# A fused attention, mixture-of-experts and bilinear kernel: heads grouped as 4 g + j, fewer small vector operations, and the attention's stores moved from SyncE's queue to ScalarE's

## The chip, the cores and the metric

The kernel runs on one core of one Trainium2 chip. The metric is the device time of one execution in microseconds (us). All tensors stay in the chip's memory; there is one launch. The core has five engines that run their own instruction streams in order: PE (TensorE), DVE (VectorE), ACT (ScalarE), POOL (GpSimd) and SP (SyncE, which issues DMAs and computes nothing). ACT and POOL can issue DMAs too; an issue stands in the stream of the engine that makes it.

## The reference, cut to what matters

Three stages follow one another; the diff touches the first.

```python
# 1. attention between x (8 batches, 8 heads, 512 rows, 64) and state (8, 8, 32, 64), both ways
scores = x @ state.T / 8;      xread = softmax(scores) @ state      # softmax over the 32 state rows
scores2 = state @ x.T / 8;     sread = softmax(scores2) @ x         # softmax over the 512 x rows
rows = concat([xread, sread], axis=2).transpose(0, 2, 1, 3).reshape(8 * 544, 512)   # heads side by side
# 2. mixture of experts: 8 experts, top 1, d_model 512, d_ff 1024
logits = rows @ w_gate;  e = argmax(logits);  p = softmax(logits)[e];  g = sigmoid(rows @ w_output_gate)[e]
y = p * g * (relu(rows @ w1[e]) @ w2[e])
# 3. bilinear layer
out = ((y @ wa) * (y @ wb)) @ w3 @ w_out
```

A softmax divides by its sum plus 1e-9.

## The kernel before

**Layout.** The 8 heads are split as h = 2 j + g, with g in 0..1 and j in 0..3: 4 heads of one g stand on the 128 partitions as 4 groups of 32 state rows. `st_n` holds the state so, `stT` its transposes, and `st_d` a block-diagonal form of it with 2 x 8 gate columns at its end, so that one product gives a row's attention result and its gate logits at once.

**One batch** is made of two functions. `softmaxes(b)` transposes x (PSUM tiles `pxT`, copied to `xT`), makes both score matrices (`psT`, taken over to `sT` with a running maximum `m2e`), transposes the scores (`pS`), subtracts the maximum of each 32 (`m1`, giving `a`), takes the exponentials (`a` and `a2`, both on ACT), sums them (`s1`, `s2`) and inverts the sums (`s1`, `r2`); POOL multiplies `a` by `s1` into `an`. `read(b)` transposes `a2` and `an` (`pa2T`, `paT`, copied to `a2T`, `aT`), makes the state's read (`psr`, scaled by `r2` into `sr`, stored to `x_rows`) and, for 4 chunks of 128 rows and 2 values of g, one product `pxr` of 272 columns: 256 are the attention result, copied to `xr` and stored, and 16 are logits, copied (g = 0) or added (g = 1) into `L` by DVE.

**What else runs beside it.** The weights `w3` and `w_out` arrive as 64-bit floats and are turned into 32-bit words by `convert`: ACT (L225, L239), DVE (L228, L230, L233) and POOL (L240); the raw words have a ring of 3 buffers (`RAW = 3`). Then `fuse` multiplies w3 by w_out, a block of 128 rows at a time: transposes `pw3`, split into a high and a low part (`w3T0`, `w3T1`), 24 products `pwo`. Blocks 0 to 2 are fused inside the attention, 3 to 7 beside the routing, where POOL makes the low parts.

**After the attention**, `route` (DVE, some 100 small operations) turns the logits `L` into expert slots and places; its first product is `pc`. POOL then gathers rows of `x_rows` (`xg`, L997), which are transposed (`pxg`) and go into the first expert unit (`ph4`, tiles 20 to 23).

**What sets the order.** A scheduler that is part of the language orders each engine's instructions from its own forecast of times, and picks the engine of an operation that is marked `any`: the copies `xr` (all of them), `xT` (three of four), and `aT`, `a2T` (one piece of the four) are so marked; the others are fixed. So an edit moves copies between ACT and DVE without the diff saying so. `bank` gives PSUM tiles from three tags, A (4), B (2) and C (2).

Lines of the profile before: L140 is `cp` (all copies), L548 `psT`, L556 the take-over of `sT`, L600, L606, L607 the small steps around `r2`, L632 `psr`, L654 `pxr`, L660 and L662 the logits, L643 and L663 the two stores, L328 the load of x, L208 the load of raw weights, L183 the products of `fuse` and of all later stages.

Of the kernel before, what the change touches and what calls it, by code (L numbers as in the profile page):

```python
# [52 lines left out]
def tile_attention_moe_bilinear(  # L53
# [256 lines left out]
    with ExitStack() as c1:  # L310
# [12 lines left out]
        def load_x(b):  # L323

            t = xin.tile([P, H, NC_, D], F32, tag="x", name=f"x{b}")
            for j in range(NJ):
                h = slice(2 * j, 2 * j + 2)
                eng("q_x", j, "sync").dma_start(  # L328
                    out=t[:, h].rearrange("p h c d -> p h (c d)"),
                    in_=x[b, h].rearrange("h (p c) d -> p h (c d)", c=NC_),  # L330
                )
            x_t[b] = t
# [4 lines left out]
        def load_state(b, n, qs):  # L337
            for h in range(H):
                j, g = divmod(h, 2)
# [29 lines left out]
        nc.scalar.dma_start(out=wg[:, :, 0:E], in_=w_gate.rearrange("(k p) e -> p k e", p=P))  # L369
        nc.scalar.dma_start(out=wg[:, :, E:], in_=w_ogate.rearrange("(k p) e -> p k e", p=P))  # L370
# [10 lines left out]
        def spread_state(b, n):  # L381
            for h in range(H):
                j, g = divmod(h, 2)
# [140 lines left out]
        def softmaxes(b):  # L524
# [3 lines left out]
            for j in range(NJ):  # L528
# [12 lines left out]
            s2 = two.tile([P, 2], F32, tag="s2", name=f"s2{b}")  # L541
            r2 = two.tile([P, 2], F32, tag="r2", name=f"r2{b}")

            t = [bank((kn("t_psT", "B")*4)[e], f"psT{b}_{e}") for e in range(2)]
            for j in range(NJ):
                for g in range(2):
                    for e in range(2):
                        nc.tensor.matmul(  # L548
                            t[e][at(j), g * S // 2 : (g + 1) * S // 2], stT[e ^ g][of(e), b, at(j)],
                            xT[of(e), 2 * j + g, :], start=True, stop=True,  # L550
                        )
            if kn("m2", 1):
                m2e = two.tile([P, 2, 2], F32, tag="m2e", name=f"m2e{b}")
                for g in range(2):
                    for e in range(2):
                        nc.vector.tensor_scalar(  # L556
                            sT[:, g].rearrange("p (c e n) -> p c e n", e=2, n=P)[:, :, e, :],
                            t[e][:, g * S // 2 : (g + 1) * S // 2].rearrange("p (c n) -> p c n", n=P),
                            1.0, None, op0=ALU.mult, op1=ALU.max, accum_out=m2e[:, e, g : g + 1],
                        )  # L560
                nc.vector.tensor_tensor(m2, m2e[:, 0], m2e[:, 1], op=ALU.max)
            else:
                for e in range(2):
                    cp(
                        "e_sT", e, sT.rearrange("p g (c e n) -> p g c e n", e=2, n=P)[:, :, :, e, :],
                        t[e].rearrange("p (g c n) -> p g c n", g=2, n=P),
                    )
                for g in range(2):
                    nc.vector.tensor_reduce(m2[:, g : g + 1], sT[:, g, :], axis=AX.X, op=ALU.max)
# [3 lines left out]
            for g in range(2):  # L573
                t = bank((kn("t_pS", "B")*4)[g], f"pS{b}_{g}")
                for c in range(NC_):
# [4 lines left out]
                nc.vector.tensor_reduce(m1[:, g], tv, axis=AX.X, op=ALU.max)  # L580
                nc.vector.tensor_tensor(
                    a[:, g], tv, m1[:, g].unsqueeze(2).to_broadcast([P, NC_ * NJ, NS]),
                    op=ALU.subtract,
                )
            av = a.rearrange("p g h n -> p (g h) n")
            nc.scalar.activation(av, av, AF.Exp, scale=SCALE)
            s1 = two.tile([P, 2 * NC_ * NJ], F32, tag="s1", name=f"s1{b}")
            nc.vector.tensor_reduce(s1, av, axis=AX.X, op=ALU.add)
# [3 lines left out]
            for g in range(2):  # L592
                eng("e_an", g, "gpsimd").tensor_tensor(
                    an[:, g].rearrange("p c (j n) -> p (c j) n", n=NS), a[:, g],
                    s1[:, g * NC_ * NJ : (g + 1) * NC_ * NJ]
# [3 lines left out]
            nm2 = two.tile([P, 2], F32, tag="nm2", name=f"nm2{b}")  # L599
            nc.vector.tensor_scalar_mul(nm2, m2, -SCALE)  # L600
            for g in range(2):
                nc.scalar.activation(
                    a2[:, g, :], sT[:, g, :], AF.Exp, bias=nm2[:, g : g + 1], scale=SCALE,
                    accum_out=s2[:, g : g + 1],
                )
            nc.vector.tensor_scalar_add(r2, s2, 1e-9)  # L606
            nc.vector.reciprocal(r2, r2)  # L607
# [15 lines left out]
        def read(b):  # L623
# [4 lines left out]
            for g in range(2):  # L628
                a2T = transposed(f"a2T{b}_{g}", [a2[:, g, c * P : (c + 1) * P] for c in range(NC_)], g)
                for c in range(NC_):  # L630
                    for j in range(NJ):
                        nc.tensor.matmul(  # L632
                            t[at(j), of(g)], a2T[:, c, at(j)], xt[:, 2 * j + g, c, :],
                            start=(c == 0), stop=(c == NC_ - 1),
                        )
            if b % 4 == 0:
# [6 lines left out]
            eng("q_sr", 0, "sync").dma_start(  # L643
                out=x_rows[b * R + S : (b + 1) * R, :].rearrange("n (j f) -> j n f", j=NJ), in_=sr
            )

            aT = [transposed(f"aT{b}_{g}", [an[:, g, c, :] for c in range(NC_)], 2 + g) for g in range(2)]
            xo = x_rows[b * R : b * R + S, :].rearrange("(p c) f -> c p f", c=NC_)
            for c in range(NC_):
                xr = xin.tile([P, DM], F32, tag="xr", name=f"xr{b}_{c}", bufs=kn("b_xr", 3))  # L650
                logits = L[:, b * NC_ + c]
                for g in range(2):
                    t = bank((kn("t_pxr", "CB")*8)[2 * c + g], f"pxr{b}_{c}_{g}")[:, 0 : NJ * D + 2 * E]
                    nc.tensor.matmul(t, aT[g][:, c, :], st_d[:, b % (B // 2), g], start=True, stop=True)  # L654
# [919 lines left out]
```

## Time and profile before

| | |
|---|---|
| median of 3 runs | 1168.14 us (1165.36 to 1170.16) |
| the profiled execution | 1171.04 us, its span 1169.1 us |
| PE busy | 1118.7 us (96%) |
| DVE, ACT, POOL busy | 664.0, 450.7, 398.2 us |
| granted TensorE clock, mean | 0.99 |

The span runs from the first to the last instruction of one execution. An engine is busy while it runs an instruction; the time in which an instruction waits inside itself counts as busy too. In a group of instructions the second last figure is the busy time and the mean of one in ns, the last the idle time just before them and what ended most of it.

### The profile page before, as it was taken

The numbers are of one execution on the slowest core, as the hardware profiler recorded it, in microseconds if no ns is written. First come the engines' busy times: TensorE is split into PE (matmuls) and PEld (weight loads), VectorE is DVE, ScalarE is ACT, GpSimd is POOL, SyncE is SP. The second block draws the span as 40 slices with busy tenths as digits, with TensorE's granted clock in tenths as the row PEclk, the third lists the DMA queues.
The fourth block names the chain that finished last, engine by engine and source line by source line (L and its number), as shares of the span: only waits on it lengthen the run. The fifth ranks groups of instructions, "written<-read, shape, count | busy, mean of one in ns | idle before, by whom it ended". The sixth has DMA issues, their size and how long they took to land. (4 is left out here: it accounts for less than half of the span.)

```text
span 1169.1 us, 18224 instructions
## 1 busy us (share of the span) xinstructions
PE 1118.7 (96%) x6880; PEld 982.7 (84%) x6880; DVE 664.0 (57%) x1206; ACT 450.7 (39%) x807; POOL 398.2 (34%) x383
## 2 busy tenths in 40 slices
PE   6888998999999999999999999999999999999995
PEld 4666777999999999987888888898888889889994
DVE  4999787636464546464855547343644545463341
ACT  3778644435454545454413223121412322131121
POOL 2555326114140322132001434623543453344222
PEclk9899999999999999999999999999999999999998
DMA  7786425546566666677414645443544445343431
GB/s 227 223 254 200 160 96 209 201 153 228 187 228 211 215 216 201 233 221 242 158 35 176 248 152 199 171 174 141 205 174 160 156 180 189 135 181 132 184 127 57
DMA packets 85008, 211.55 MB, mean 181 GB/s; under 512 B 12976, under 2 KB 42672, under 8 KB 79920
## 3 DMA queue, kind: packets, MB, share of 16 engines
q1 hardware_dynamic: 62256, 167.53, 42.2%
q10 hardware_dynamic: 17024, 24.42, 5.7%
q0 software_dynamic: 5632, 18.35, 4.5%
q8 instruction: 56, 0.92, 0.3%
q14 instruction: 40, 0.33, 0.1%
HBM read 166.23 MB, written 44.04 MB: 180 GB/s over the span
## 5 line engine op out<-in xcount | busy, mean ns | idle before, releaser
L183 PE MATMUL p<-w_x,w 128*128 128x448 f32 (+1 forms) x1638 | 338.6, 360 | 0.0
L183 PEld LDWEIGHTS p<-w_x,w 128*128 128x128 f32 x1638 | 303.7, 188 | 25.4
L183 PE MATMUL py<-h,w 128*128 128x288 f32 (+1 forms) x1152 | 197.9, 329 | 3.0 <-ACT y L1087 3.0
L183 PE MATMUL ph<-x,w 128*128 128x288 f32 (+2 forms) x1248 | 196.5, 316 | 2.9 <-DVE h L1025 2.7
L183 PEld LDWEIGHTS ph<-x,w 128*128 128x128 f32 x1248 | 179.4, 188 | 15.6 <-DVE h L1025 4.4
L183 PEld LDWEIGHTS py<-h,w 128*128 128x128 f32 x1152 | 173.8, 188 | 19.2 <-ACT y L1087 4.6
L178 DVE TENSOR_TENSOR w<-raw,w 128x1024 fp32r<-128x1024 f32 x80 | 96.9, 1237 | 74.6 <-ACT w L177 72.5
L1434 POOL TENSOR_TENSOR ab<-u,s 128x448 f32<-128x448 f32 (+1 forms) x40 | 47.6, 1189 | 259.3 <-DVE u L1432 170.4
L183 PE MATMUL po<-w_wo,aa 128*128 128x512 f32 x480 | 125.3, 393 | 1.9 <-ACT aa L177 1.0
L183 PEld LDWEIGHTS po<-w_wo,aa 128*128 128x128 f32 x480 | 89.7, 188 | 18.8 <-DVE aa L178 1.7
L177 ACT CAST w<-raw 128x1024 fp32r<-128x1024 f32 x80 | 81.6, 1050 | 51.6 <-DMA raw<-in_moe_w 46.8
L177 ACT CAST ab<-ab 128x384 fp32r<-128x384 f32 (+1 forms) x40 | 19.7, 493 | 184.4 <-POOL ab L1440 174.0
L240 POOL TENSOR_TENSOR wab<-wab,wab_top 128x512 int32<-128x512 int32 x16 | 20.7, 1292 | 179.5 <-DVE wab_top L233 151.5
L183 PE MATMUL po<-w_wo,ab 128*128 128x512 f32 x336 | 79.6, 391 | 0.4 <-DVE o L1466 0.4
L183 PEld LDWEIGHTS po<-w_wo,ab 128*128 128x128 f32 x336 | 62.9, 188 | 13.9 <-DVE o L1466 0.8
L997 POOL DMA_INDIRECT xg<-x_rows,gidx x38 | 45.7, 1202 | 83.3 <-PE pxg L1003 66.7
L1437 DVE TENSOR_TENSOR u<-u,p 128x448 f32<-128x448 f32 (+1 forms) x40 | 24.3, 606 | 84.4 <-PE p L183 84.3
L1438 POOL TENSOR_TENSOR ab<-u,s 128x448 f32<-128x448 f32 (+1 forms) x40 | 48.3, 1208 | 49.2 <-DVE u L1437 49.2
L1025 DVE SCALAR_TENSOR_TENSOR h<-ph,h 128x288 fp32r<-128x288 f32 (+2 forms) x104 | 51.2, 502 | 20.8 <-ACT h L1024 20.3
L1024 ACT ACTIVATE h<-ph 128x288 fp32r<-128x288 f32 (+2 forms) x104 | 44.5, 447 | 42.6 <-PE ph L183 30.8
L183 PE MATMUL pwo<-wu,w3T 128*128 128x512 f32 x192 | 50.2, 411 | 3.4 <-POOL w3T L178 2.9
L1440 POOL TENSOR_TENSOR ab<-ab 128x448 f32<-128x448 f32 (+1 forms) x40 | 48.9, 1222 | 3.1
(291 smaller groups left out, 1441.0 us busy)
## 6 DMA issues: line engine op xcount, KB each, us to landing
w<-w_rows SPq DMA_DIRECT2D x39, 1792.0 KB
raw<-in_moe_w SPq DMA_DIRECT2D x80, 512.0 KB
x<-in_x SPq DMA_DIRECT2D x32, 256.0 KB
w_raw<-in_moe_w SPq DMA_DIRECT2D x16, 512.0 KB
x_rows<-xr SPq DMA_DIRECT2D x32, 256.0 KB
w_rows<-wh_s ACTq DMA_DIRECT2D x32, 256.0 KB
y<-y_T SPq DMA_DIRECT2D x8, 896.0 KB
w_rows<-wh_w ACTq DMA_DIRECT2D x32, 192.0 KB
```

The lines of the kernel that those rows point to most:

```text
L177: nc.scalar.copy(hi, src)
L178: (engine or nc.vector).tensor_tensor(lo, src, hi.bitcast(F32), op=ALU.subtract)
L183: m = nc.tensor.matmul(o, l[a], r[b], start=start and i == 0, stop=stop and i == 2)
L240: nc.gpsimd.tensor_tensor(wi, wi, top, op=ALU.add)
L997: gathered = nc.gpsimd.indirect_dma_start(out=x[0:r], out_offset=None, in_=x_rows, in_offset=bass.IndirectOffsetOnAxis(ap=gidx[0:r, t - s0 ...
L1024: nc.scalar.activation(hl[0], src, AF.Relu)
L1025: nc.vector.scalar_tensor_tensor(out=hl[1], in0=src, scalar=0.0, in1=hl[0].bitcast(F32), op0=ALU.max, op1=ALU.subtract)
L1434: gpsimd(b2, u3, s5, op=ALU.add)
L1437: vector(u4, u2, p3, op=ALU.add)
L1438: gpsimd(a2, u4, s5, op=ALU.add)
L1440: gpsimd(ab[:, n : 2 * n], a2, b2, op=ALU.mult)
```

## The change

1. Heads are split as h = 4 g + j. The results of one g are then 256 neighbouring columns of a row. x is loaded and transposed in the order of head pairs 0, 2, 1, 3; the gate weights come in 4 DMAs in place of 2.
2. The take-over of `sT` multiplies by -1/8 and takes the minimum, so the separate negation (`nm2`, L600) is gone, and the sums of both softmaxes share one tile `s1` of 34 columns: the separate add and reciprocal (L606, L607) are gone. The exponentials of `a2` stand ahead of those of `a`.
3. The copy of `pxr` takes all 272 columns. The logits of two chunks are then added by one DVE operation from `xr` (16 in all, in place of 64 from PSUM). A `xr` tile holds two chunks (2 buffers in place of 4).
4. The stores of `sr` (two per batch, 256-byte pieces, in place of one with 512-byte pieces) and of `xr` (still one per chunk, but as two pieces of 1 KB per row in SBUF) are issued by ACT in place of SP.

```diff
-            for j in range(NJ):
-                h = slice(2 * j, 2 * j + 2)
+            for i in (0, 2, 1, 3):
+                h = slice(2 * i, 2 * i + 2)
...
-                j, g = divmod(h, 2)
+                g, j = divmod(h, NJ)
...
                     for e in range(2):
                         nc.vector.tensor_scalar(
...
-                            1.0, None, op0=ALU.mult, op1=ALU.max, accum_out=m2e[:, e, g : g + 1],
+                            -SCALE, None, op0=ALU.mult, op1=ALU.min, accum_out=m2e[:, e, g : g + 1],
...
+            s1 = two.tile([P, 2 + 2 * NC_ * NJ], F32, tag="s1", name=f"s1{b}")
+            for g in range(2):
+                nc.scalar.activation(
+                    a2[:, g, :], sT[:, g, :], AF.Exp, bias=m2[:, g : g + 1], scale=-1.0,
+                    accum_out=s1[:, g : g + 1],
+                )
             av = a.rearrange("p g h n -> p (g h) n")
-            nc.scalar.activation(av, av, AF.Exp, scale=SCALE)
...
+            nc.scalar.activation(av, av, AF.Exp)
+            nc.vector.tensor_reduce(s1[:, 2:], av, axis=AX.X, op=ALU.add)
             nc.vector.tensor_scalar_add(s1, s1, 1e-9)
             nc.vector.reciprocal(s1, s1)
...
-            nc.vector.tensor_scalar_mul(nm2, m2, -SCALE)
...
-            nc.vector.tensor_scalar_add(r2, s2, 1e-9)
-            nc.vector.reciprocal(r2, r2)
+            r2 = s1[:, 0:2]
...
-            eng("q_sr", 0, "sync").dma_start(
-                out=x_rows[b * R + S : (b + 1) * R, :].rearrange("n (j f) -> j n f", j=NJ), in_=sr
-            )
+            for g in range(2):
+                nc.scalar.dma_start(
+                    out=x_rows[b * R + S : (b + 1) * R, :].rearrange(
+                        "n (g j d) -> g j n d", g=2, j=NJ
+                    )[g],
+                    in_=sr[:, of(g)],
+                )
...
-                    cp(
-                        "e_xr", 2 * c + g, xr.rearrange("p (j g d) -> p g j d", g=2, d=D)[:, g],
-                        t[:, 0 : NJ * D].rearrange("p (j d) -> p j d", d=D),
-                    )
-                    if g == 0:
-                        nc.vector.tensor_copy(logits, t[:, NJ * D :])
-                    else:
-                        nc.vector.tensor_tensor(logits, logits, t[:, NJ * D :], op=ALU.add)
-                eng("q_xr", c, "sync").dma_start(out=xo[c], in_=xr)
+            for c0 in range(0, NC_, 2):
+                xr = xin.tile([P, 2, 2, NJ * D + 2 * E], F32, tag="xr", name=f"xr{b}_{c0}", bufs=2)
+                for i in range(2):
+                    for g in range(2):
...
+                        cp("e_xr", g, xr[:, i, g], t)
+                for i in range(2):
+                    nc.scalar.dma_start(out=xo[:, c0 + i], in_=xr[:, i, :, 0 : NJ * D])
+                nc.vector.tensor_tensor(
+                    L[:, b * NC_ + c0 : b * NC_ + c0 + 2, :], xr[:, :, 0, NJ * D :],
+                    xr[:, :, 1, NJ * D :], op=ALU.add,
+                )
```

The scheduler's order moves with it. Three places follow. In a row stand the line, the operation, what it writes and reads, and the shape; a number behind a name is the batch (and piece).

**Place 1, the middle of the attention (batch 3).** On DVE before, around the sum of the exponentials of batch 4 (`s14`), the logits of batch 3 are taken from PSUM 16 columns at a time:

```order
L588 TENSOR_REDUCE s14_1167<-a4_1150 128x32
L233 SCALAR_TENSOR_TENSOR wu_7_top_1082<-wu_7_raw_1080,wu_7_top_1082 128x512
L228 TENSOR_SCALAR w3_2_0_top_1183<-w3_2_0_top_1183 128x512
L662 TENSOR_TENSOR L_75<-L_75,pxr3_0_1_1268 128x16
L662 TENSOR_TENSOR L_75<-L_75,pxr3_1_1_1278 128x16
L589 TENSOR_SCALAR s14_1167<-s14_1167 128x32
L660 COPY L_75<-pxr3_2_0_1284 128x16
L230 TENSOR_SCALAR w3_2_0_top_1183<-w3_2_0_top_1183 128x512
L660 COPY L_75<-pxr3_3_0_1294 128x16
L590 RECIPROCAL s14_1167<-s14_1167 128x32
```

On DVE now, at the same place:

```order
L140 COPY xT5_1275<-pxT5_2_1282 128x512
L140 COPY xr3_0_1215<-pxr3_0_1_1219 128x272
L588 TENSOR_REDUCE s14_1121<-a4_1105 128x32
L140 COPY xT5_1275<-pxT5_1_1288 128x512
L140 COPY xr3_0_1215<-pxr3_0_0_1216 128x272
L228 TENSOR_SCALAR w3_2_1_top_1144<-w3_2_1_top_1144 128x512
L140 COPY xr3_0_1215<-pxr3_1_0_1222 128x272
L589 TENSOR_SCALAR s14_1121<-s14_1121 128x34
L228 TENSOR_SCALAR w3_3_0_top_1356<-w3_3_0_top_1356 128x512
L230 TENSOR_SCALAR w3_2_1_top_1144<-w3_2_1_top_1144 128x512
L656 TENSOR_TENSOR L_75<-xr3_0_1215 128x32
L590 RECIPROCAL s14_1121<-s14_1121 128x34
```

Five small operations on `L` around the sum have given way to one, and DVE makes three copies `xr` of 272 columns and two copies `xT` there, most of which were ACT's before. Over the whole program DVE now has 26 copies `xr` (3 before), 16 `xT` (10), 15 `aT` and `a2T` (9), and 16 additions into `L` (64 operations before); ACT has 38 `xr` (61), 16 `xT` (22), 17 `aT` and `a2T` (23). On ACT now, at that place, stores stand between copies and conversions:

```order
L140 COPY xT5_1275<-pxT5_0_1276 128x512
L636 DMA x_rows_68<-sr0_494 4x32x64 x2
L225 ACTIVATE w3_3_0_top_1356<-w3_3_0_raw_1354 128x512
L239 ACTIVATE w3_3_0_1353<-w3_3_0_raw_1354 128x512
L140 COPY xr3_0_1215<-pxr3_1_1_1225 128x272
L140 COPY srT0_1262<-psrT0_1257 128x512
L140 COPY xT5_1275<-pxT5_3_1294 128x512
L140 COPY xr3_2_1231<-pxr3_2_1_1235 128x272
L655 DMA x_rows_68<-xr3_0_1215 128x2x256 x2
L239 ACTIVATE w3_3_1_1363<-w3_3_1_raw_1364 128x512
```

No store stood on ACT in the attention before; SP's queue there now has loads alone, in nearly the same order.

**Place 2, PE at the first product of the routing (`pc`).** Before, two of the last twelve products of fuse block 2 (`pwo2`, second half, from `w3T0_2_1` and `w3T1_2_1`) stand ahead of it and ten behind:

```order
L183 MATMUL pwo2_2201<-wu0_181,w3T0_2_1_2228 128x512
L183 MATMUL pwo2_2201<-wu1_182,w3T0_2_1_2228 128x512
L752 LDWEIGHTS ones_81
L752 MATMUL pc_2276<-cnt_2274,ones_81 128x8
L753 LDWEIGHTS before_208
L753 MATMUL pc_2276<-cnt_2274,before_208 128x8
L458 MATMUL pw33_0_2488<-ident_70,w3_3_0_1415 128x128 x4
L458 MATMUL pw33_1_2511<-ident_70,w3_3_1_1425 128x128 x4
L458 MATMUL pw34_0_2538<-ident_70,w3_4_0_1435 128x128 x2
L183 MATMUL pwo2_2201<-wu0_181,w3T1_2_1_2229 128x512
```

Now all twelve stand ahead; the last three are shown:

```order
L183 MATMUL pwo2_2099<-wu0_183,w3T0_2_1_2126 128x512
L183 MATMUL pwo2_2099<-wu1_184,w3T0_2_1_2126 128x512
L183 MATMUL pwo2_2099<-wu0_183,w3T1_2_1_2127 128x512
L748 LDWEIGHTS ones_81
L748 MATMUL pc_2174<-cnt_2172,ones_81 128x8
L749 LDWEIGHTS before_210
L749 MATMUL pc_2174<-cnt_2172,before_210 128x8
L463 MATMUL pw33_0_2386<-ident_70,w3_3_0_1353 128x128 x4
```

From the end of the attention (`psl1`) to `pc` PE has 48 products of fuse blocks 1 and 2, where it had 38.

**Place 3, PE at the first expert unit.** Before, the transposes of gathered tile 21 stand behind two products of the second half of fuse block 7 (`w3T0_7_1`), so behind the twelve of its first half:

```order
L183 MATMUL pwo7_2687<-wu0_181,w3T0_7_1_2716 128x512
L183 MATMUL pwo7_2687<-wu1_182,w3T0_7_1_2716 128x512
L1003 MATMUL pxg21_2854<-ident_70,xg21_2852 128x128 x4
L183 MATMUL pwo7_2687<-wu0_181,w3T1_7_1_2717 128x512
L183 MATMUL pwo7_2687<-wu0_181,w3T0_7_1_2716 128x512
```

Now they stand behind two products of its first half, right after those of tile 20:

```order
L999 MATMUL pxg20_2743<-ident_70,xg20_2741 128x128 x4
L183 MATMUL pwo7_2585<-wu0_183,w3T0_7_0_2591 128x512
L183 MATMUL pwo7_2585<-wu1_184,w3T0_7_0_2591 128x512
L999 MATMUL pxg21_2752<-ident_70,xg21_2750 128x128 x4
L183 MATMUL pwo7_2585<-wu0_183,w3T1_7_0_2592 128x512
```

Ten products of that block now stand behind the unit's first products `ph4`. From there on PE's order is the same but for a few neighbours that changed places.

## Rows read from the trace of the kernel before

**Rows 1.** Busy time by stretch (stretch, length, engines, PE clock, DMA share, GB/s).

```profile
40.00:76.00 36.00, 31.13 (x352) 21.56 (x333) 36.00 (x102) 28.60 (x62) 20.31 (x18) 1.00 0.80 250
76.00:112.00 36.00, 31.49 (x403) 23.25 (x404) 35.97 (x99) 28.96 (x63) 18.83 (x17) 1.00 0.71 221
...
124.00:146.00 22.00, 21.86 (x245) 17.87 (x244) 15.58 (x48) 15.50 (x35) 6.43 (x6) 1.00 0.41 140
146.00:183.00 37.00, 34.36 (x191) 26.65 (x190) 30.83 (x100) 15.26 (x26) 10.98 (x7) 1.00 0.23 85
183.00:200.00 17.00, 14.71 (x67) 11.45 (x65) 12.39 (x31) 7.99 (x13) 12.35 (x9) 0.90 0.75 270
200.00:300.00 100.00, 99.39 (x703) 94.47 (x702) 51.66 (x85) 46.95 (x87) 24.23 (x28) 1.00 0.59 196
```

**Rows 2.** DVE's groups from 28 to 130 us, shapes apart.

```profile
L228 DVE TENSOR_SCALAR w_top<-w_top 128x512 f32<-128x512 f32 x15 | 9.0, 600 | 0.0
...
L140 DVE COPY xT<-pxT 128x512 f32<-128x512 f32 x8 | 5.4, 678 | 0.5 <-PE pxT L532 0.5
...
L606 DVE TENSOR_SCALAR r<-s 128x2 f32<-128x2 f32 x6 | 3.5, 586 | 0.0
...
L662 DVE TENSOR_TENSOR L<-L,pxr 128x16 f32<-128x16 f32 x24 | 3.4, 152 | 0.0
L660 DVE COPY L<-pxr 128x16 f32<-128x16 f32 x24 | 3.4, 161 | 0.0
...
L600 DVE TENSOR_SCALAR nm<-m 128x2 f32<-128x2 f32 x7 | 1.8, 254 | 0.0
...
L140 DVE COPY xr<-pxr 128x256 f32<-128x256 f32 x3 | 1.2, 405 | 0.0
L607 DVE RECIPROCAL r<-r 128x2 f32<-128x2 f32 x6 | 0.9, 150 | 0.0
```

**Rows 3.** Order of time around 51 us, POOL and DVE (start, length).

```profile
50.60 1.27 POOL L240 TENSOR_TENSOR w<-w,w_top 128x512 int32<-128x512 int32 x1 [2.31 <-DVE w_top L233]
...
50.65 0.68 DVE L140 COPY aT<-paT 128x512 f32<-128x512 f32 x1
...
51.25 0.66 DVE L606 TENSOR_SCALAR r<-s 128x2 f32<-128x2 f32 x1
...
51.82 0.41 DVE L228 TENSOR_SCALAR wu_top<-wu_top 128x512 f32<-128x512 f32 x1
```

**Rows 4.** ACT's groups from 28 to 130 us.

```profile
L140 ACT COPY xr<-pxr 128x256 f32<-128x256 f32 x45 | 15.8, 384 | 2.4 <-PE pxr L654 2.1
...
L140 ACT COPY xT<-pxT 128x512 f32<-128x512 f32 x16 | 9.5, 592 | 0.0
```

**Rows 5.** SP's issues in order of time: a load of x, a store of sr, one of xr.

```profile
48.44 1.50 SPq L328 DMA_DIRECT2D x<-in_x  x3
50.75 0.56 SPq L643 DMA_DIRECT2D x_rows<-sr  x1
...
123.59 0.38 SPq L663 DMA_DIRECT2D x_rows<-xr  x1
```

**Rows 6.** ACT and PE in order of time at the end of the first pause.

```profile
26.21 0.66 ACT L225 ACTIVATE wu_top<-wu_raw 128x512 f32<-128x512 f32 x1 [5.83 <-DMA wu_raw<-in_moe_w_out]
...
28.58 1.06 ACT L140 COPY a2T<-pa2T 128x512 f32<-128x512 f32 x2
...
29.20 1.94 PE L632 MATMUL psr<-x,a2T 128*32 128x64 f32 x64 [4.96 <-ACT a2T L140]
```

**Rows 7.** DVE in order of time in the last batch.

```profile
133.96 0.34 DVE L590 RECIPROCAL s<-s 128x32 f32<-128x32 f32 x1
```

**Rows 8.** PE and DVE in order of time at the first product of the routing.

```profile
145.91 9.08 PE L183 MATMUL pwo<-wu,w3T 128*128 128x512 f32 x38
...
155.07 0.17 DVE L758 TENSOR_SCALAR nq<-pc 128x8 int32<-128x8 f32 x1 [1.80 <-PE pc L753]
```

**Rows 9.** PE in order of time ahead of the first expert unit.

```profile
192.95 4.22 PE L183 MATMUL pwo<-wu,w3T 128*128 128x512 f32 x12 [2.16 <-POOL w3T L178]
```

More of the change, by code (lines that the diff above doesn't have):

```diff
@@ L382, in spread_state @@
             for h in range(H):
-                j, g = divmod(h, 2)
+                g, j = divmod(h, NJ)
                 i = b % (B // 2)
@@ L527, in softmaxes @@
             xT = two.tile([P, H, S // 2], F32, tag="xT", name=f"xT{b}", bufs=kn("b_xT", 1))
-            for j in range(NJ):
+            for j in (0, 2, 1, 3):
                 t = bank((kn("t_pxT", "A")*4)[j], f"pxT{b}_{j}")
@@ L549, in softmaxes @@
                             t[e][at(j), g * S // 2 : (g + 1) * S // 2], stT[e ^ g][of(e), b, at(j)],
-                            xT[of(e), 2 * j + g, :], start=True, stop=True,
+                            xT[of(e), NJ * g + j, :], start=True, stop=True,
                         )
[L552 to L558, printed above, removed]
-                            1.0, None, op0=ALU.mult, op1=ALU.max, accum_out=m2e[:, e, g : g + 1],
-                        )
-                nc.vector.tensor_tensor(m2, m2e[:, 0], m2e[:, 1], op=ALU.max)
-            else:
+            m2e = two.tile([P, 2, 2], F32, tag="m2e", name=f"m2e{b}")
+            for g in range(2):
                 for e in range(2):
-                    cp(
-                        "e_sT", e, sT.rearrange("p g (c e n) -> p g c e n", e=2, n=P)[:, :, :, e, :],
-                        t[e].rearrange("p (g c n) -> p g c n", g=2, n=P),
-                    )
-                for g in range(2):
-                    nc.vector.tensor_reduce(m2[:, g : g + 1], sT[:, g, :], axis=AX.X, op=ALU.max)
+                    nc.vector.tensor_scalar(
+                        sT[:, g].rearrange("p (c e n) -> p c e n", e=2, n=P)[:, :, e, :],
+                        t[e][:, g * S // 2 : (g + 1) * S // 2].rearrange("p (c n) -> p c n", n=P),
+                        -SCALE, None, op0=ALU.mult, op1=ALU.min, accum_out=m2e[:, e, g : g + 1],
+                    )
+            nc.vector.tensor_tensor(m2, m2e[:, 0], m2e[:, 1], op=ALU.min)
             a = two.tile([P, 2, NC_ * NJ, NS], F32, tag="a", name=f"a{b}", bufs=kn("b_a", 1))
@@ L632, in read @@
                         nc.tensor.matmul(
-                            t[at(j), of(g)], a2T[:, c, at(j)], xt[:, 2 * j + g, c, :],
+                            t[at(j), of(g)], a2T[:, c, at(j)], xt[:, NJ * g + j, c, :],
                             start=(c == 0), stop=(c == NC_ - 1),
@@ new lines, in read @@
+            for g in range(2):
+                nc.scalar.dma_start(
+                    out=x_rows[b * R + S : (b + 1) * R, :].rearrange(
[3 more added lines that the diff above has]
+                )
+            aT = [transposed(f"aT{b}_{g}", [an[:, g, c, :] for c in range(NC_)], 2 + g) for g in range(2)]
+            xo = x_rows[b * R : b * R + S, :].rearrange("(p c) (g f) -> p c g f", c=NC_, g=2)
+            for c0 in range(0, NC_, 2):
+                xr = xin.tile([P, 2, 2, NJ * D + 2 * E], F32, tag="xr", name=f"xr{b}_{c0}", bufs=2)
+                for i in range(2):
+                    for g in range(2):
+                        t = bank("CB"[g], f"pxr{b}_{c0 + i}_{g}")[:, 0 : NJ * D + 2 * E]
+                        nc.tensor.matmul(
+                            t, aT[g][:, c0 + i, :], st_d[:, b % (B // 2), g], start=True, stop=True
+                        )
+                        cp("e_xr", g, xr[:, i, g], t)
[4 more added lines that the diff above has]
+                    xr[:, :, 1, NJ * D :], op=ALU.add,
+                )
```

33 lines of the change are left out of this document (7 added, 26 removed).

## The prediction

> **What bounds the kernel now.** I read the busy time by stretch first. From 200 us on PE is busy for 99.39 of 100 us [rows 1], and it has the same products to do there before and after; so the question is at which moment PE gets there. In the attention another engine is full: from 40 to 112 us DVE is busy for 71.97 of 72 us, ACT for 57.6, POOL for 39.1, and PE has gaps [rows 1]. DVE runs in order and never pauses there, so whatever its instructions take in this loop sets when the logits are complete. From 124 to 146 us DVE is busy for only 15.58 of 22 us [rows 1]: the last two batches are a chain of waits. From 146 us the routing runs on DVE (30.83 of 37 us) while PE still fuses (34.36 of 37 us) [rows 1]: two nearly full chains side by side, so a delay in one can be partly taken up by the other.
>
> Secondly I read DVE's groups in that loop, for the prices. One point about them: neighbours overlap a little. A copy of 512 columns starts at 50.65 and takes 0.68, and the next instruction starts at 51.25 [rows 3]; so each costs its mean less 0.08 us.
>
> **DVE's loop, 28 to 130 us.** Removed: 24 copies of logits at 161 ns and 24 additions at 152 ns, 1.9 + 1.7 us; the two small steps around the second softmax's sum, 6 x 0.51 and 6 x 0.07 us; the negation, 7 x 0.17 us; three copies xr, 3 x 0.325 us [rows 2]. Together 9.3 us. (Two batches' logits lie behind 130 us.)
>
> Added, by the new order: 18 copies xr of 272 columns (of 26; eight lie in the last batches). At 256 columns one takes 405 ns [rows 2]; in proportion 430, so 0.35 us each, 6.3 us. Ten more copies of 512 columns, xT, aT and a2T, at 678 ns [rows 2], 0.60 each, 6.0 us (of 12; one stands ahead of the loop, one behind). And 12 additions into L, two operands in SBUF, 32 columns, which the trace does not show. From below such a small operation costs 0.08 us like a copy of logits; from above 0.51 like the step L606. The nearest is L600, also tiny and on SBUF alone, 254 ns or 0.17 [rows 2]: I take that, 2.0 us (1.0 to 6.1). Sum 14.3 us, net **+5.0 us**; the bounds of the additions make it +4.0 to +9.1.
>
> One thing could move this. L606 works on two columns, yet takes 586 ns in the mean, and its sister L607 150 [rows 2]. Around 51 us one sees why: POOL's L240 runs from 50.60 to 51.87; L606 starts at 51.25 and ends at 51.91, just after it, and the step L228 behind it then takes its short 0.41; the copy from PSUM at 50.65 ran beside POOL at its usual length [rows 3]. L228 has 600 ns in the mean [rows 2], so it meets such waits too. If the wait is POOL's to give, removing L606 leaves it to the next instruction of that kind: 6 x 0.44 for L606 and 7 x 0.10 for L600, 3.3 us of what I counted as removed would stay. The Trainium skill, SBUF — State Buffer, "Who interferes with whom", says just this: DVE and GpSimd share a port pair as an exclusive lock; tensor_scalar in a two-port mode, and any DVE instruction with two SBUF inputs against a GpSimd instruction that reads SBUF, blocks until the other ends. The trace agrees at 51.91. By that rule the loop's net is +8.3 us; by the rows taken alone +5.0. On the other side, a copy from PSUM that falls under a POOL instruction eats up a wait that would have come behind it. The two pull against each other, so I keep +5.0 and leave both as rivals.
>
> **ACT.** It gives away 23 copies xr at 384 ns and 12 of 512 columns at 592 [rows 4], 15.9 us in all eight batches. It gains 48 issues. A store of xr is now 128 x 2 pieces, the shape in which x is loaded: 0.50 us an issue; the store of sr took 0.56, the old store of xr 0.38 [rows 5]. 32 x 0.50 + 16 x 0.56 makes 25 us, so ACT gains 9 us over some 120: from 80% busy [rows 1] to under 90. DVE's fullness covers that, so I count nothing. Without this cover: a store waits in ACT's stream for DVE (the product sr, the copies xr), and behind it stand conversions (L225, L239) whose results DVE's L228 and L233 need. Half a us in each of eight batches would be 4 us.
>
> **SP and the DMAs.** SP loses 40 issues, and its loads no longer stand behind a store that waits for a copy. Earlier weights help ACT alone, and DVE would still be full: nothing. The smaller pieces of the stores are needed only by POOL's gathers, 40 us after the last store: nothing. The two extra gate DMAs stand ahead of anything ACT could do: nothing.
>
> **The first pause.** ACT waits 5.83 us for raw weights, does four conversions, and only then copies a2T, from 28.58; PE's psr starts at 29.20 [rows 6]. Now the first a2T stands after two of the four and the second is DVE's. PE can start about 1.2 us earlier; since DVE is full soon after I take **-0.7 us** (0 to -1.2).
>
> **The last batch.** Between the sum s1 and its reciprocal, which ends at 134.3 [rows 7], DVE now has four copies xr of batch 6 and one addition in place of two small steps: 4 x 0.35 + 0.17 less some 0.3 us, +1.3 us on the way to POOL's product an. Sharing the evictions of the last batches between two engines gives some back. I take **+1.0 us** (0 to +3).
>
> **The routing and the first expert unit.** To reach pc PE has 48 fuse products in place of 38. The 38 took 9.08 us [rows 8], 0.239 each, so pc comes 2.4 us later against the logits, and DVE, which waited 1.80 us for it [rows 8], would wait 4.2; the slots and gathers come 2.4 us later. But that fuse work is then done, and PE no longer keeps tile 21 behind a product that waits for POOL: there it paused 2.16 us, and the next twelve products took 4.22 us, 0.35 each, in a stretch whose granted clock is 0.90 [rows 1, 9]. At 0.239 each they take 2.9. That is at most 3.5 us back. I take **-1.0 us** (-3.5 to +2.4).
>
> **Sum.** -0.7 + 5.0 + 1.0 - 1.0 = +4.3 us. The profiled execution took 1171.04 us, 2.9 more than the median of the three runs, 1168.14; the difference is added to the median: **1172.4 us**. A measurement of this kernel can tell about 0.5%, 5.8 us, from no change, and the forecast is inside that.
>
> **Rivals.**
> *The waits stay and ACT's stores reach DVE (slower).* The 3.3 us stay, which gives +7.6; with half a us a batch from stores that wait in ACT's stream, +11.6: 1176 to 1180 us. For it: row 51.91; a full DVE makes what waits for it late. Against: ACT has a fifth of its time free. Chance 0.35.
> *The added copies run inside POOL's waits (faster).* POOL is busy in 39 of 72 us [rows 1], copies from PSUM ran beside it at full length, and 12.3 us of such copies are added. Every us of them that lies where DVE would have waited costs nothing. Half of that makes the sum -1.9, not to be told from no change; the kernel is faster by over 0.5% from 10.1 us on, and with all of them it ends near 1160. For it: waits are many. Against: a copy helps only if one of the blocked kind stands right behind it. Chance 0.13.
> *DVE's load does not carry over.* The loop grows, but PE's fuse work in the routing takes the delay up, since it has its own 34 us to do there; 1167 to 1169. Against it: the logits are first in the route's chain. Chance 0.12.
> The forecast itself, +1 to +5.8, has 0.40.
>
> **How the numbers follow.** Slower by over 0.5%: the first rival, 0.35. Faster: the second, 0.13. Within: the forecast and the third, 0.52. Below 1163 lie most of the second rival, above 1181 the upper bounds of the additions and stores together, about one in ten each: the range is 1163 to 1181. The forecast's own is 1169 to 1174.
>
> **What would show it.** DVE full from 28 to 130 us and beyond, the first fuse product behind the logits near 151 us in place of 145.91 [rows 8]; 26 copies xr near 430 ns; the additions L656 near 250 ns; the mean of L228, L561 and L589 grown where waits moved, shrunk where copies swallowed them; ACT near 88% in the loop; DVE's wait for pc near 4 us. Wrong would be: pauses on DVE in the loop with ACT as releaser, or a loop that ends no later than before.

## The result, and the profile after

The changed kernel took 1177.27 us (median of 5 runs, 1176.65 to 1178.18), the kernel before 1168.63 beside it: 1.0073 times as long, interval 1.0058 to 1.0088, so 8.6 us slower. The forecast was 1172.4, range 1163 to 1181; the kernel before was measured again in every later call, with medians of 1166.37 to 1167.26. The profiled execution of after took 1178.18 us, its span 1176.3.

Busy time by stretch, columns as in [rows 1]:

```profile
40.00:76.00 36.00, 30.62 (x329) 21.20 (x326) 35.20 (x77) 24.25 (x50) 20.78 (x18) 0.95 0.78 245
76.00:112.00 36.00, 32.13 (x316) 23.66 (x316) 33.82 (x76) 22.16 (x45) 17.52 (x16) 0.86 0.64 195
...
183.00:200.00 17.00, 14.53 (x92) 11.00 (x91) 14.62 (x49) 6.27 (x11) 11.25 (x8) 0.90 0.37 125
200.00:300.00 100.00, 96.33 (x645) 89.24 (x644) 54.78 (x86) 48.13 (x85) 24.25 (x28) 0.97 0.60 199
```

DVE is no longer quite full from 40 to 112 us (69.02 of 72); the pauses that the profile names from 28 to 130 us, 2.6 us, end with PE (2.4) and ACT (0.2). ACT is busy for 46.4 of 72 us, 64%. The 88% that I had named can't be read here: it counted the issues, 25 us over 120, and the profile doesn't count an issue as busy; without them it was 67%. PE's granted clock, 1.00 before [rows 1], is 0.95 and 0.86. From 200 us PE, which before was busy for 99.39 of 100 us, has 96.33.

DVE's groups from 28 to 130 us, shapes apart, beside [rows 2]:

```profile
L233 DVE SCALAR_TENSOR_TENSOR wu_top<-wu_raw,wu_top 128x512 int32<-128x512 int32 x8 | 9.2, 1144 | 0.0
L140 DVE COPY xT<-pxT 128x512 f32<-128x512 f32 x13 | 8.6, 678 | 0.3 <-PE pxT L537 0.3
L140 DVE COPY xr<-pxr 128x272 f32<-128x272 f32 x18 | 7.4, 424 | 0.0
L228 DVE TENSOR_SCALAR w_top<-w_top 128x512 f32<-128x512 f32 x14 | 6.1, 438 | 0.0
L656 DVE TENSOR_TENSOR L<-xr 128x32 f32<-128x32 f32 x12 | 5.2, 431 | 0.3 <-ACT xr L140 0.2
...
L589 DVE TENSOR_SCALAR s<-s 128x34 f32<-128x34 f32 x6 | 1.1, 178 | 0.0
```

The copies have the forecast price (424 ns against 430, 678 as before). The additions L656 took 431 ns in place of 254; among the conversions the L228 shown shrank from 600 to 438, and the L233 shown grew from 854 to 1144; L589 shrank from 569 to 178.

Four places in order of time. First ACT and PE at the end of the first pause, then on DVE the last batch's sum, its reciprocal and the last write into `L`, then DVE behind the first product of the routing, then PE at the first expert unit ([rows 6, 7, 8, 9] before):

```profile
24.61 0.66 ACT L225 ACTIVATE wu_top<-wu_raw 128x512 f32<-128x512 f32 x1 [5.04 <-DMA wu_raw<-in_moe_w_out]
...
26.35 1.94 PE L624 MATMUL psr<-x,a2T 128*32 128x64 f32 x64 [4.19 <-ACT a2T L140]
...
139.54 1.21 DVE L588 TENSOR_REDUCE s<-a 128x32 f32<-128x1024 f32 x1
...
142.39 0.35 DVE L590 RECIPROCAL s<-s 128x34 f32<-128x34 f32 x1
...
153.07 0.17 DVE L669 COPY L<-psl 128x16 f32<-128x16 f32 x1
...
163.68 0.17 DVE L754 TENSOR_SCALAR nq<-pc 128x8 int32<-128x8 f32 x1 [4.12 <-PE pc L749]
...
199.47 0.68 PE L999 MATMUL pxg<-ident,xg 128*128 128x128 f32 x4 [2.47 <-DMA xg<-x_rows,gidx]
199.88 1.13 PE L183 MATMUL pwo<-wu,w3T 128*128 128x512 f32 x2
202.83 1.09 PE L999 MATMUL pxg<-ident,xg 128*128 128x128 f32 x4 [1.82 <-DMA xg<-x_rows,gidx]
203.57 4.51 PE L183 MATMUL pwo<-wu,w3T 128*128 128x512 f32 x12
207.92 0.64 PE L183 MATMUL ph<-x,w 128*128 128x256 f32 x4
...
225.15 11.78 PE L183 MATMUL ph<-x,w 128*128 128x256 f32 x96 [1.48 <-DVE h L1021]
236.76 0.63 PE L183 MATMUL py<-h,w 128*128 128x512 f32 x2
```

Three of these marks in the kernel before, which its rows do not show:

```profile
132.13 1.22 DVE L588 TENSOR_REDUCE s<-a 128x32 f32<-128x1024 f32 x1 [0.46 <-ACT a L586]
...
146.10 0.17 DVE L673 COPY L<-psl 128x16 f32<-128x16 f32 x1 [0.34 <-PE psl L670]
...
225.21 6.99 PE L183 MATMUL py<-h,w 128*128 128x512 f32 x30
```

PE reaches psr 2.85 us earlier, the last batch's sum starts 7.4 us later (132.13 before), the logits are complete 7.0 us later (153.24 against 146.27, the end of the last write into `L`), PE's first fuse product behind the attention starts at 152.19 (145.91 before [rows 8], forecast near 151), DVE has pc 8.6 us later, after the wait of 4.12 us that was forecast (near 4). At the unit the expected return is not there: PE waits for the gathers of tiles 20 and 21, 2.47 and 1.82 us, and the next twelve products take 4.51 us at a mean granted clock of 0.64, as slowly as before (4.22 us [rows 9], 0.68). The unit starts 7.4 us later, but ten products of block 7 still stand inside it, and before its last products `ph` PE pauses another 1.48 us. The first product `py` behind them is a better mark, since all fuse products lie ahead of it in both kernels: 236.76 against 225.21 before, 11.55 us later.

### The profile page after: what moved, and what is told of

Its sections match the earlier page's. It is cut to its first block, busy times and chain, and to the rows that moved or that the text cites. A ratio compares the mean times of both kernels' runs of the same rounds, so it can differ in the third digit from the quotient of the medians.

```text
span 1176.3 us, 18147 instructions
## 1 busy us (share of the span) xinstructions
PE 1126.6 (96%) x6880; PEld 989.1 (84%) x6880; DVE 673.1 (57%) x1169; ACT 437.5 (37%) x772; POOL 395.9 (34%) x383
## 5 line engine op out<-in xcount | busy, mean ns | idle before, releaser
L183 PEld LDWEIGHTS po<-w_wo,ab 128*128 128x128 f32 x336 | 62.9, 188 | 13.3 <-ACT o L1460 0.3
L993 POOL DMA_INDIRECT xg<-x_rows,gidx x38 | 41.7, 1096 | 87.2 <-PE pxg L999 81.3
```

Of the source, the lines that this page charges most:

```text
L183: m = nc.tensor.matmul(o, l[a], r[b], start=start and i == 0, stop=stop and i == 2)
L993: gathered = nc.gpsimd.indirect_dma_start(out=x[0:r], out_offset=None, in_=x_rows, in_offset=bass.IndirectOffsetOnAxis(ap=gidx[0:r, t - s0 ...
```

## The experiments

Ahead of the expectations one table of all runs, so that they can be read against each other. "xr" and "512" are the copies that DVE makes (of 64 each); "products" those of `pwo` between `psl1` and `pc`. Then, from the profiled execution, the end of the last write into `L`, how far behind it `pc` and the first `py` start, and the start of that `py`; then the median, what it is above that of before in the same call, and the ratio to before with its interval. The ratio is estimated from all runs of both kernels, so it need not be the quotient of the medians; they differ most in e9 (8.6 us against 0.56%, 6.5 us).

```
run   stores xr 512 products logits    pc     py      py at   median  over   ratio (interval)
before  SP    3  19   38     146.27   8.56   78.94   225.21
after   ACT  26  31   48     153.24  10.20   83.52   236.76  1177.27  8.6  1.0073 (1.0058-1.0088)
e1      SP    0  21   48     152.62  10.55   83.17   235.79  1176.57  9.3  1.0080 (1.0065-1.0096)
e2      ACT  15  26   38     152.43   8.56   78.32   230.75  1173.11  5.9  1.0066 (1.0048-1.0083)
e3      ACT   0  16   48     146.08  10.89   83.56   229.64  1174.06  6.8  1.0065 (1.0047-1.0083)
e4      SP    3  23   48     145.62  10.70   85.49   231.11  1170.95  3.7  1.0030 (1.0014-1.0046)
e5      SP    0  16   48     146.19  10.55   83.55   229.74  1173.50  6.4  1.0058 (1.0043-1.0073)
e6      ACT   0  16   48     145.34  10.89   83.39   228.73  1171.78  4.6  1.0039 (1.0023-1.0055)
e7      SP    1  24   38     151.75   8.56   79.22   230.97  1172.06  4.9  1.0046 (1.0029-1.0063)
e8      ACT  18  33   48     148.82   9.21   85.41   234.23  1174.13  7.0  1.0063 (1.0048-1.0078)
e9      SP    2  17   48     150.22  10.54   83.44   233.66  1174.93  8.6  1.0056 (1.0037-1.0076)
e10     ACT   0  16   38     150.74   8.57   79.13   229.87  1172.74  6.4  1.0052 (1.0031-1.0073)
e11     SP    0  16   38     148.39   8.45   79.01   227.40  1168.47  2.1  1.0014 (0.9999-1.0029)
e12     SP    0  16   38     147.88   8.55   77.61   225.49  1168.34  2.0  1.0022 (1.0004-1.0039)
```

From that `py` to its end a profiled execution took 937.3 to 943.9 us, without any order by kernel; before, with 943.9, was the longest. So a mark of one execution and a median can differ by some 3 us, and both are given.

### The queue, and the copies that move with it: e1, e2, e3, e5, e10

e1 is the changed kernel with the stores on SP, e2 the kernel before with the stores on ACT:

```diff
-                nc.scalar.dma_start(
+                nc.sync.dma_start(
...
-                    nc.scalar.dma_start(out=xo[:, c0 + i], in_=xr[:, i, :, 0 : NJ * D])
+                    nc.sync.dma_start(out=xo[:, c0 + i], in_=xr[:, i, :, 0 : NJ * D])
```

> The changed kernel with all stores back on SP's queue, nothing else edited. In the scheduler's order DVE then has no copy xr (26 in the changed kernel), 9 xT (16) and 12 aT and a2T (15). Theory 1, the loss is the copies that the scheduler moved to DVE because it charges ACT for the issues: 26 copies at 0.335 us and 10 of 512 columns at 0.60 leave DVE's loop, 14.7 us, against 6.6 us more of DVE work in the changed kernel than before; the loop then ends ahead of the one before and the time is 1163 to 1168 us. Theory 2, the loss is ACT's stream itself, held up by stores: the same kernel gains 7 to 9 us, 1168 to 1170 us. Theory 3, the loss is the thinner operations (additions L656 that wait, later pc): 1174 to 1178 us.

> The kernel before with its stores of sr and xr issued by ACT, nothing else edited. The scheduler then gives DVE 15 copies xr (3 before) and 26 of 512 columns (19 before). Theory 1 (moved copies): 12 x 0.33 + 7 x 0.60 = 8.2 us more DVE work in a full loop, 1174 to 1178 us. Theory 2 (stores hold up ACT's stream): slower too, 1173 to 1178 us, with ACT pauses behind its stores. Theory 3 (the thinner operations are the loss): 1167 to 1170 us.

e1 took 1176.57: DVE lost all copies xr and nothing came back, so my theory 1 fell as it stood; the time lies in the range of theory 3, but e2, below, does not. I counted, from 28 us to the logits, the shortest time of each instruction's own form in its run, and apart from it what each took beyond that. By this estimate DVE's bare work was 86.1 us before, 93.8 after and 82.0 in e1, and the time beyond it 25.0, 22.4 and 29.6; other ways to count the overlap of neighbours move these figures by up to 3 us. DVE's idle time was 7.2, 8.9 and 13.5 us. So of the 12 us or so that e1 took from DVE some 7 came back as waits inside instructions and 4.6 as pauses. DVE's additions L656 and the step L589 in e1, from 28 to 130 us:

```profile
L656 DVE TENSOR_TENSOR L<-xr 128x32 f32<-128x32 f32 x11 | 7.3, 668 | 1.0 <-ACT xr L140 1.0
...
L589 DVE TENSOR_SCALAR s<-s 128x34 f32<-128x34 f32 x6 | 3.8, 627 | 0.0
```

In after they took 431 and 178 ns: without the copies around them, more of POOL's time falls on these. Of all 16 additions in e1, the eight that start while an instruction of POOL runs take 965 ns in the mean, the other eight 183. e2 was slower (1173.11, at the low end of theory 2's range and 0.9 us below theory 1's), so it doesn't tell these two apart; theory 3 had it at 1167 to 1170.

e3 leaves the stores on ACT and fixes the engines of the copies; e5 is e3 with the stores on SP, e10 the kernel before with e3's fixed copies and its stores on ACT:

```diff
-'ahead': 1,
+'ahead': 1, 'e_xr': 'scalar',
...
-'e_tr': ['scalar', 'any', 'any', 'vector']
+'e_tr': ['scalar', 'scalar', 'scalar', 'vector']
...
-'e_xT': ['any', 'any', 'vector', 'any']
+'e_xT': ['scalar', 'scalar', 'vector', 'scalar']
```

> The changed kernel with its stores still on ACT, but the copies xr fixed to ACT, and xT, aT, a2T fixed so that DVE has one piece in four of each pair of rows, as nearly as before the change (8 xT, 8 aT). Theory 1 (moved copies are the loss, and an issue runs beside ACT's instructions): DVE loses the 14.7 us, the time falls to 1163 to 1169 us. Theory 2 (the stores cost ACT its time: 48 issues of about 0.5 us, 25 us over 120 us, on an engine that was busy for 57.6 of 72 us): ACT becomes the full engine and the time stays at 1177 us or rises to 1185. Theory 3: 1174 to 1178 us.

> The run with the copies fixed to ACT (e3) with its stores back on SP's queue: the same copies on the same engines, so only the queue differs. Theory Q, a store that waits in ACT's stream for DVE holds up the copies and conversions behind it: 1166 to 1170 us, 4 to 8 us less than e3. Theory O, the queue costs nothing by itself, what counts is where the scheduler puts DVE's conversions and PE's pauses: 1172 to 1177 us, like e3 (1174.06).

> The kernel before with its stores on ACT (e2), and the copies fixed as in e3, so that none can move to DVE; the routing keeps its 38 products ahead of pc. Theory M, the queue costs nothing and the moved copies are all that e2 lost: logits near 146 us, 1166 to 1169 us, no change against before. Theory Q, stores in ACT's stream cost: 1171 to 1175 us.

With the copies fixed the logits are back at 146.08 (stores on ACT) and 146.19 (on SP), and the medians are 6.8 and 6.4 us over before: in the changed kernel the queue alone moves neither. `py` comes 7.1 us earlier than in after, but the median against before came down by only 1.8 us, not by the 8 to 14 expected: the marks of one execution make the copies look dearer than the medians do, and most of the loss lies elsewhere. e10 missed theory M: 1172.74, logits at 150.74. I made no run with fixed copies alone on the kernel before, so whether its queue or the fixing cost those 4.5 us stays open; in e11, below, the same fixing with the stores on SP came with logits 2.8 us later than in e4.

Why an issue costs ACT so little is seen in after, ACT in order of time ("ACTq" is an issue):

```profile
39.85 0.68 ACT L140 COPY xr<-pxr 128x272 f32<-128x272 f32 x2
40.27 0.41 ACTq L655 DMA_DIRECT2D x_rows<-xr  x1
40.41 0.41 ACT L140 COPY xr<-pxr 128x272 f32<-128x272 f32 x1
40.78 0.43 ACTq L655 DMA_DIRECT2D x_rows<-xr  x1
```

The issue runs from 40.27 to 40.68, within it one copy ends and the next begins. That the queue alone moves copies is shown: 26 copies xr leave DVE in e1, 12 come to it in e2. That the scheduler does so because it charges ACT for the issues is my reading of it. A store that waits can hold up ACT, though: at 74.56 one waits for a copy xr of DVE, which ends at 77.23 behind a conversion, and ACT's next instruction starts at 77.68. The profile puts the end of that wait down to another instruction of DVE, so what part of the 3.98 us is the store's is not shown:

```profile
72.89 0.81 ACT L140 COPY xr<-pxr 128x272 f32<-128x272 f32 x2 [0.39 <-DVE w_top L233]
74.56 3.07 ACTq L655 DMA_DIRECT2D x_rows<-xr  x2
77.68 0.68 ACT L225 ACTIVATE wu_top<-wu_raw 128x512 f32<-128x512 f32 x1 [3.98 <-DVE sT L558]
```

### The additions: e6, e7, e8

e6 is e3, and e7 is e1, with the logits from PSUM as before the change; e8 is the changed kernel with the additions on POOL:

```diff
-                        cp("e_xr", g, xr[:, i, g], t)
+                        cp("e_xr", g, xr[:, i, g, 0 : NJ * D], t[:, 0 : NJ * D])
+                        logits = L[:, b * NC_ + c0 + i]
+                        if g == 0:
+                            nc.vector.tensor_copy(logits, t[:, NJ * D :])
+                        else:
+                            nc.vector.tensor_tensor(logits, logits, t[:, NJ * D :], op=ALU.add)
...
-                nc.vector.tensor_tensor(
-                    L[:, b * NC_ + c0 : b * NC_ + c0 + 2, :], xr[:, :, 0, NJ * D :],
```

> The run with the copies fixed to ACT (e3), but the logits taken from PSUM 16 columns at a time as before the change (64 operations of DVE in place of 16 additions L656, copies xr of 256 columns). Theory L, the additions from two operands in SBUF are a cost of their own since they wait for POOL (2.4 us of such waits in e3, 4.3 in the changed kernel, 6.3 in e1): 1169 to 1172 us. Theory O: 64 operations at 0.10 us, 6.6 us, take the place of 16 at 0.38, 6.0 us, and the time stays at 1172 to 1177 us.

> The changed kernel with its stores back on SP's queue (e1) and the logits taken from PSUM as before the change. In the scheduler's order PE has 38 fuse products ahead of pc again (48 in e1) and 130 between pc and the first expert unit (110). Theory L, the additions' 6.3 us of waits in e1: 1170 to 1172 us; with the routing's place on top of it, 3 us: 1167 to 1169 us. Theory O, both change nothing for the chain from psT to sT: 1173 to 1178 us.

> The changed kernel with the 16 additions into L made by POOL in place of DVE; stores on ACT, copies as the scheduler likes. POOL is busy for 38 of 72 us from 40 to 112 us, so it has room. Theory L: DVE gets back 6.0 us, 4.3 us of it waits: 1170 to 1174 us. Theory O: the waits pass to the next instruction of DVE that POOL blocks, and the time stays at 1175 to 1179 us.

e6 (1171.78), e7 (1172.06) and e8 (1174.13) all came out at the upper edge of theory L; in e7 the routing's return, which had 1167 to 1169 with theory L, is in that time already. The logits came 0.7, 0.9 and 4.4 us earlier; the medians against before fell by 2.2, 4.4 (with the routing's return) and 1.6 us. So the additions cost some 1 to 2 us where DVE has no copies xr, about the least that the intervals can tell; in e8, whose order also left DVE only 18 of them, up to 4.4 at the logits. In e3, in the same stretch, they took what I had predicted:

```profile
L656 DVE TENSOR_TENSOR L<-xr 128x32 f32<-128x32 f32 x12 | 3.1, 258 | 0.7 <-ACT xr L140 0.7
```

### One copy: e9

e1 and e5 have nearly the same copies on DVE, yet their logits are 6.4 us apart. e9 takes from e1 the copies a2T on DVE (`'e_tr': ['scalar', 'scalar', 'any', 'vector']`).

> The run with the stores on SP (e1) with one more edit: the second copy a2T of each batch is fixed to ACT. In e1 DVE made 4 of the 16; it now has 2 copies xr, 9 xT, 8 aT and no a2T, nearly the same as in e5 (0, 8, 8, 0), whose logits were complete at 146.19 us against 152.62 in e1. Theory D, a copy a2T that stands in DVE's stream behind conversions is what keeps PE's psr and all behind it late: logits near 146 us, time 1171 to 1174 us like e5. Theory O, it is not one copy but the whole order that the scheduler wrote around it (conversions ahead of the take-over of sT, PE's pauses, the slower clock behind them): logits stay at 151 to 153 us, 1175 to 1178 us.

1174.93 us, logits at 150.22: between the two theories, 2.4 of the 6.4 us. Theory D explains the smaller part; what in the order makes up the rest is not shown.

### The routing's place: e4, e11, e12

e4 is the kernel before with the softmax part of the diff alone; e11 is e4 with e3's fixed copies; e12 is e6 with the stores on SP. In e11 and e12 the scheduler, not an edit of mine, puts 38 products ahead of pc and 130 between pc and the unit; in e4 and e6 it had 48 and 110.

> The kernel before with the softmax part of the change alone (one sum tile s1, the negation inside the take-over of sT, a2's exponentials ahead of a's); stores on SP, logits from PSUM. Removed from DVE's loop are L600, L606 and L607, 4.8 us with their waits. If the time of these steps is their own (no wait passes to another): 1163 to 1166 us. If POOL's waits pass to the next instruction of the blocked kind, 3.3 us of it stay: 1166 to 1168 us. If the order of the two exponentials delays an, or the routing loses its place: 1168 to 1172 us.

> The kernel before with the thin softmax (e4) and the copies fixed as in e3; stores on SP, logits from PSUM. The scheduler then leaves the routing as before the change (38 products ahead of pc, 130 between pc and the first expert unit; 48 and 110 in e4). Theory R, e4 lost by the routing's place alone, some 4 us from pc to the first expert unit, while its logits were 0.6 us earlier: 1164 to 1168 us, perhaps the fastest. Theory S, the thin softmax itself costs: 1169 to 1172 us.

> The run with copies fixed to ACT and logits from PSUM (e6) with its stores on SP. The copies stand where they did; what differs in the order beside the queue is the routing: 38 products ahead of pc in place of 48, 130 in place of 110 ahead of the first expert unit. Theory R: e6 (1171.78) less 3 to 5 us, 1166 to 1169 us, pc 8.6 us behind the logits in place of 10.9. If the routing's place costs nothing: 1170 to 1173 us.

The column "py" sorts all kernels: 77.6 to 79.2 us from the logits to `py` in the six with 38 products, 83.2 to 85.5 in the eight with 48, whatever else they do. PE's pauses sort them too: from `pc` to `py` they make 4.9 to 6.3 us in the six and 8.4 to 11.0 in the eight, while PE is busy there for 63.4 to 65.4 us in all; the mean granted clock there is 0.98 to 1.00 in the six, 0.91 to 0.95 in the eight. e4 took 1170.95 although its logits were 0.65 us earlier than before. e11 and e12 are 2.1 and 2.0 us over before where their partners were 3.7 and 4.6, although their logits came 2.8 and 2.5 us later; e12 came out by theory R, e11 (1168.47) between R and S. e6, DVE at pc and PE at the unit:

```profile
144.98 11.41 PE L183 MATMUL pwo<-wu,w3T 128*128 128x512 f32 x48
...
156.47 0.17 DVE L755 TENSOR_SCALAR nq<-pc 128x8 int32<-128x8 f32 x1 [4.13 <-PE pc L750]
...
194.95 0.96 PE L1000 MATMUL pxg<-ident,xg 128*128 128x128 f32 x4 [3.29 <-DMA xg<-x_rows,gidx]
195.56 4.39 PE L183 MATMUL pwo<-wu,w3T 128*128 128x512 f32 x12
```

and e12:

```profile
147.51 9.08 PE L183 MATMUL pwo<-wu,w3T 128*128 128x512 f32 x38
...
156.67 0.17 DVE L755 TENSOR_SCALAR nq<-pc 128x8 int32<-128x8 f32 x1 [1.83 <-PE pc L750]
...
194.82 3.06 PE L183 MATMUL pwo<-wu,w3T 128*128 128x512 f32 x12 [1.82 <-POOL w3T L178]
197.72 0.60 PE L1000 MATMUL pxg<-ident,xg 128*128 128x128 f32 x4
```

With 48 ahead, DVE waits 2.3 us longer for pc. Of this the first gather keeps 1.3 us: it starts 40.2 us behind the logits in e6, 38.9 in e12. PE, which has spent those products, then stands before tile 21 for 3.29 us, and the next twelve run at a mean granted clock of 0.66. With 38 ahead PE has the products to run, tile 21 is there when PE comes, the pause behind POOL is 1.82 us, and the twelve run at 1.00. No run changes the routing's place alone: in e11 the copies are fixed as well, in e12 the queue is another. No version beat the kernel before; e11 can't be told from it. As a ladder by medians: after 8.6 us over before, copies fixed 6.8 (e3), logits from PSUM 4.6 (e6), the routing's old place and the stores on SP 2.0 (e12). Each ratio is known to about 2 us, so a single step is less sure than the whole, and the last 2.0 no run takes apart.

## Why the prediction was right in its range and wrong in its sum

Rival A below is the prediction's first rival, rival B its second. The range held, but that says little for the sum: it spanned the forecast and both of these rivals. The time fell where rival A had it, 1176 to 1180 us, by a path of which A had only a part, so that is luck too.

*First pause* (-0.7): -2.85 at psr, outside my bounds. The raw weights were there 1.6 us earlier (24.61 against 26.21 [rows 6]), which I had counted as nothing. There is no sign that it brought anything: e5 and e6 reach psr 2.1 and 2.9 us earlier than before and have their logits 0.1 and 0.9 us earlier.

*DVE's loop* (+5.0): as a count this was close. From 28 us to the logits DVE was busy for 111.1 us before and 116.3 after. The terms inside were off both ways: L656 cost 0.38 us without the overlap in place of 0.17, over 16 of them some 3.4 us more; the time beyond bare work fell, by the estimate above, from 25.0 to 22.4 us. So most of the waits stayed, as rival A had it, and some 2.6 us went, which is the size of a small part of rival B. What failed is the sentence "whatever its instructions take in this loop sets when the logits are complete". e1, e5 and e6 took 12 to 15 us of bare work from DVE against after; the logits moved by 0.6 us in e1, by 7 to 8 in the others, and in those DVE idles for 11 us and more. The loop is a chain through DVE, PE, ACT and the weight loads, in which a full DVE is one link; so its size can't be had from DVE's count alone. From psr to the last sum it grew by 10.3 us.

*The lower clock* was no term of mine. Before, it was 1.00 from 40 us to the logits. In after, PE pauses in front of `pS`, and the clock is half (1.2 GHz) behind the pauses: nothing of PE from 56.2 to 59.9 us, half the clock after it, and again around 77 us; a third time from 94.2 us, behind a pause of 1.87 us.

```profile
56.20:59.90 3.70, 0.00 (x0) 0.00 (x0) 3.70 (x8) 1.49 (x3) 2.49 (x3) 1.00 0.63 210
60.10:63.30 3.20, 3.20 (x15) 3.02 (x16) 2.98 (x10) 0.98 (x2) 2.08 (x2) 0.50 0.61 181
...
75.30:77.50 2.20, 0.00 (x0) 0.00 (x0) 2.20 (x6) 0.00 (x0) 1.50 (x2) 0.91 0.94 330
77.70:80.40 2.70, 2.70 (x13) 2.53 (x14) 2.50 (x11) 1.75 (x3) 0.59 (x1) 0.50 0.80 192
```

In both pauses PE waits for the take-over `sT`, and DVE, ahead of it in its order, runs conversions that wait for POOL (from 75.49 an L233 of 1.40 us). From 28 us to the logits, before and after:

```profile
28.00:146.27 118.27, 105.02 (x1170) 77.42 (x1171) 111.06 (x297) 91.09 (x196) 59.02 (x50) 0.96 0.66 207
28.00:153.24 125.24, 112.47 (x1121) 82.10 (x1114) 116.32 (x256) 77.10 (x159) 58.77 (x50) 0.91 0.63 196
```

PE's pauses in sum did not grow, 13.3 and 12.8 us, as far as its records, of which a few per cent can be missing, show; its busy time grew by 7.5 us at the lower clock. So the clock may carry much of the 7 us. It does not sort the runs, though: from 40 to 146 us it was 1.00 in e10, whose logits came at 150.74, and 0.97 in e3, whose logits came at 146.08. No run holds the clock fixed, so whether it is a cause of the delay or comes of it stays open.

*ACT* (0): right, by e3 and e5. Rival A's second half, half a us in each batch, is not borne out there: the store at 74.56 waits as that rival said, but in the changed kernel the logits don't depend on the queue once the copies are fixed.

*Last batch* (+1.0): from the sum to its reciprocal 2.85 us in place of 1.83, +1.0 where I had +1.3, and to the logits 0.4 us less than before: some more came back than I counted.

*Routing and first unit* (-1.0): this is the step that failed, in sign. pc came 1.6 us later against the logits (forecast up to 2.4) and DVE's wait was as named, but of the 3.5 us of return none came: the pause of 2.16 us [rows 9] turned into two waits for gathers, 4.3 us, the twelve products still ran at a clock of 0.64 (0.68 before), and ten more stood inside the unit. From the logits to `py` after lost 4.6 us, and the two groups of the 14 kernels lie 5.2 us apart in the mean, 4.0 at the nearest. By the medians it is less: 1.6 us from e4 to e11 and 2.6 from e6 to e12, with logits that came later.

*Sum*: forecast -0.7 + 5.0 + 1.0 - 1.0 = +4.3. Found, up to `py`: -2.85 + 10.3 - 0.4 + 4.6 = +11.6, of which the profiled pair keeps 7.2 at its end (from there on before took longer, 943.9 against 939.5 us), and the medians 8.6. The result lies past the 0.5% that parted my forecast from rival A: up to the logits +7.0 where the terms had +5.3, and the rest is the routing, which no rival had as a loss and my own term only at its upper bound, +2.4.

Open, beside the clock: which feature of the scheduler's order makes the logits come at 146 us in e3, e5 and e6, and at 150 to 153 in e1, e7, e9 and e10, with as little work on DVE.

## What to carry to other kernels

An engine that is full in a chain of several is not yet its bound: take work from it in one run before a forecast leans on its count. Products that fill an engine's waits have two ends, as these traces show: moved ahead of a product that the critical path waits for they delay it, and they are missing at the next wait. Where a scheduler works from its own prices, look at what it moves: the queue of the stores alone parts 26 copies xr on DVE from none (after and e1).

## What the runs showed of the hardware

The same addition of 32 columns took 258, 431 and 668 ns in the mean (e3, after, e1), by what POOL did beside it: of the 16 in after, the nine that start while an instruction of POOL runs take 655 ns in the mean, the other seven 182. One of the nine, with POOL's instruction of that moment:

```profile
95.09 1.27 POOL L240 TENSOR_TENSOR w<-w,w_top 128x512 int32<-128x512 int32 x1
...
95.34 1.07 DVE L656 TENSOR_TENSOR L<-xr 128x32 f32<-128x32 f32 x1
```

It ends at 96.41, POOL's at 96.36. The Trainium skill, SBUF — State Buffer, "Who interferes with whom", has this as an exclusive lock of the port pair that DVE and GpSimd share; the trace agrees. What the runs add is that such waits do not simply go when one of the blocked instructions is taken out or made cheaper: by the estimate above, the time beyond bare work was some 18 to 30 us of DVE's 101 to 116 busy us in all 14 kernels.
